# A token product of eight blocks done with seven: sums on GpSimd, copies inside PSUM

## The chip, the cores and the metric

The kernel runs on one core of a Trainium2 chip. The metric is the device time of one execution in microseconds; the time before is the median of three runs. The profile comes from one further execution, whose times are measured by the hardware profiler: its span reaches from the first to the last instruction of the program.

## The reference

Eight batches pass through linear attention with a normalisation for each head, and then through an MLP mixer, in fp32:

```python
kv = np.einsum('bhsd,bhse->bhde', k, v)              # batch 8, heads 8, seq 576, head size 64
out = np.einsum('bhsd,bhde->bhse', q, kv)
rms = np.sqrt(np.mean(out * out, axis=-1, keepdims=True) + 1e-06)
x = (out / rms * g_norm)                             # as (batch 8, seq 576, 512)
xt = x.transpose(0, 2, 1)
h = np.maximum(xt @ w_tok1, 0.0) @ w_tok2            # w_tok1 576 x 256, w_tok2 256 x 576
u = x + h.transpose(0, 2, 1)
h2 = np.maximum(u @ w_ch1, 0.0) @ w_ch2              # w_ch1 512 x 1536, w_ch2 1536 x 512
return u + h2
```

The change touches the product `xt @ w_tok1`, the first token product. All weights arrive as 64-bit floats; the kernel turns them into fp32 on ScalarE and VectorE, which its text calls rounding.

## The kernel before

The batches are taken in four pairs. Of each pair there are nine tiles of 128 rows and 512 columns: four tiles of the first batch (side 0), four of the second (side 1), and a ninth that holds the last 64 rows of both. They are kept two by two as X[pair, c], with c from 0 to 4: X0 and X1 are side 0, X2 and X3 side 1, X4 the ninth tile. For each pair the kernel does

- **attention**: the key-value products (`kv`, evicted by ScalarE with `e`), then a product for each chunk c (`a0` to `a4`) into two PSUM banks. VectorE multiplies the banks by g_norm into X (the gain, `g`), ScalarE squares them (`q`), VectorE reduces the squares (`t`) and takes the mean (`m`), ScalarE the root (`r`), VectorE the inverse in four small steps (`i`). Then each tile is scaled by the inverse: `s` does one tile in eight ScalarE instructions, `d` one tile on VectorE (`scale_vector`), `p` one tile on GpSimd (`scale_pool`). Chunks are normalised in groups: 0 with 1, 2 with 4, and 3 alone;
- **the first token product** (`h00`, `h01`, `h10`, `h11`, function `tok1`): for each side and each half of the 256 outputs, four matmuls of 128x512 that sum over the four row tiles of that side, in a PSUM bank of pool `h` (four banks). Then `hr` (`tok1_rem`) adds the remainder's 64 rows to all four banks, and ScalarE writes the relu of each into `h1[side]`;
- **the second token product** (`u0` to `u8`, function `tok2`): two matmuls a tile. For tiles 2, 4 and 6 a bank has been seeded with x by a ScalarE copy (`z`), and the sum is copied back to x by ScalarE; for the others VectorE adds bank and x. GpSimd's queue starts the stores of the finished tiles; behind `u8` it starts three, those of the ninth tile.

The order of all this is written out by hand, as strings of step names in `middle` and `steady`, which `play` goes through. `middle` holds the attention of the second pair beside the mixing of the first; `steady[0]` and `steady[1]` hold that of the third and fourth beside the mixing of the second and third. A name with a minus belongs to the attention of the pair that is being mixed (its last chunk, `-a3`, and its last steps). A bare `1` plays the next step of the rounding of the channel weights: a clamp, a shift or an addition on VectorE, where the shift's step also issues the next block's two scaling activations on ScalarE. `f` fetches the next block of channel weights, `x` transposes finished tiles on VectorE (`turn_early`, four transposes) into parts of w_ch2 that are not filled yet, and `b` stores them; `l`, `lq` and `lr` load keys and values, queries, and their remainders on SyncE's queue.

All instructions keep the order in which the steps issue them, on each engine (`keep`). Matmuls are recorded by a helper on line 136, additions on 127, copies on 133, relus on 130; line 494 is the gain, 498 the square, 522 the reduction, 527 the mean, 532 the root, 536 to 541 the inverse, 557 the scaling on ScalarE, 566 that on VectorE, 570 that on GpSimd. Lines 181 and 186 are the scaling activations of a block of channel weights, 202, 206 and 211 clamp, shift and addition, 687 the transposes. In the changed program these lines stand one to some 95 lines further on.

Of the kernel before, what the change touches and what calls it, by code (L numbers as in the profile page):

```python
# [11 lines left out]
F32 = mybir.dt.float32  # L12
# [3 lines left out]
ALU = mybir.AluOpType  # L16
# [4 lines left out]
def kernel(  # L21
# [32 lines left out]
    nc = tc.nc  # L54
    P = 128
    B, S, DM = k.shape
    D = g_norm.shape[0]
# [13 lines left out]
    NU = B + 1  # L71
    NG = 1 + B // 2
    T = 2 * P
    assert B // 2 == 4
    EPS = 1e-6
    TOP = (2.0 - 2.0 ** -3 - 2.0 ** -23) * 2.0 ** -96

# [37 lines left out]
    def do(f, *a, **kw):  # L115
        return lambda: f(*a, **kw)
# [6 lines left out]
    def dma(o, i, engine=nc.sync):  # L123
        keep(engine.dma_start(o, i))

    def tensor_add(o, a, b, op=ALU.add, engine=nc.vector):
        keep(engine.tensor_tensor(out=o, in0=a, in1=b, op=op))  # L127

    def relu(o, a):
        keep(nc.scalar.activation(o, a, AF.Relu))  # L130

    def copy(o, a):
        keep(nc.scalar.copy(o, a))  # L133

    def matmul(*a, **kw):
        keep(nc.tensor.matmul(*a, **kw))  # L136
# [120 lines left out]
    def get_ch2(f):  # L257

        def loads(raw):
            t = raw.rearrange("p (f n) w -> p f n w", f=2)  # L260
            rows = words(moe_w_ch2)[ts(f, 2 * P)].rearrange("(f p) n w -> f p n w", f=2)
            return [(t[:, i], rows[i]) for i in range(2)]

        dst = w_ch2[:, 2 * f // NS, ds(2 * f % NS, 2)]
        return block(2 * DM, loads, dst.rearrange("p f h n -> p (f h n)"), True)
# [117 lines left out]
    def x_of(pair, i):  # L383

        return X[pair, i // 2][:, i % 2]

    def attention(pair, groups):
# [155 lines left out]
        def inv_of(c, t):  # L543

            if alone(c):
                return stat[t][2].rearrange("p (k h) o -> p k h o", h=2)
            inv = stats_of(c)[2]
            if whole:
                return inv[:, t].rearrange("p (k h) o -> p k h o", h=2)
            return inv[:, :, ts(t, HP)].rearrange("p h k o -> p k h o")  # L550
# [12 lines left out]

        def scale_vector(c, t):
            x = X[pair, c][:, t].rearrange("p (k h d) -> p k h d", h=2, d=D)
            keep(nc.vector.tensor_mul(x, x, inv_of(c, t).to_broadcast([P, HP, 2, D])))

        def scale_pool(c, t):
            x = X[pair, c][:, t].rearrange("p (k h d) -> p k h d", h=2, d=D)
# [25 lines left out]
        return steps  # L595


    def token_mixing(pair, seeds, aside=()):
        h1, acc = {}, {}

        def tok1(side, t, js=range(J)):
            if js[0] == 0:
                acc[side, t] = ps["h"].tile([P, DM], F32, name="ps_h", tag="h")
            for j in js:
                matmul(acc[side, t], lhsT=w_tok1[j // 2][:, j % 2, ts(t, P)],
                                 rhs=x_of(pair, side * J + j), start=(j == 0), stop=False)

        def tok1_rem():
            for t in range(NTOK):
                for side in range(2):  # L610
                    r = ds(side * HF, HF)
                    matmul(acc[side, t], lhsT=w_tok1r[r, ts(t, P)],
                                     rhs=x_of(pair, 8)[r], start=False, stop=True)
            for side in range(2):
                h1[side] = hp_.tile([P, NTOK, DM], F32, name="h1", tag="h1")
                for t in range(NTOK):
                    relu(h1[side][:, t], acc[side, t])

        def seed(i):


            acc[i] = ps["h"].tile([P, DM], F32, name="ps_u", tag="h")
            copy(acc[i], x_of(pair, i))

        def tok2(i):
            if i not in seeds:
                n = "o" if i in aside else "h"
                acc[i] = ps[n].tile([P, DM], F32, name="ps_u", tag=n)
            first = i not in seeds
            if i < 8:  # L630
                for t in range(NTOK):
                    matmul(acc[i], lhsT=w_tok2[:, t, ts(i % J, P)], rhs=h1[i // J][:, t],
                           start=(first and t == 0), stop=(t == NTOK - 1), skip_group_check=True)
            else:
                for t in range(NTOK):
                    for side in range(2):
                        matmul(acc[i][ds(side * HF, HF)], lhsT=w_tok2[:, t, LO:],
                               rhs=h1[side][:, t],
                               start=(first and t == 0), stop=(t == NTOK - 1), skip_group_check=True)
            x = x_of(pair, i)  # L640
            if first:
                tensor_add(x, acc[i], x)
            else:
                copy(x, acc[i])
            if i == 8:
                dma(u_rest[ts(pair, P)], x, nc.gpsimd)
                for side in range(2):
                    dma(out[2 * pair + side, LO:], x[ds(side * HF, HF)], nc.gpsimd)
            elif i % 2 == 1:
                dma(  # L650
                    u_rows(2 * pair + i // J)[ds((i % J - 1) * P, 2 * P)]
                    .rearrange("(t p) e -> p t e", p=P), X[pair, i // 2], nc.gpsimd)

        steps = {f"h{s}{t}": do(tok1, s, t) for s in range(2) for t in range(NTOK)}
        steps |= {f"h{s}{t}{j}": do(tok1, s, t, (j,)) for s in range(2) for t in range(NTOK) for j in range(J)}
        steps |= {f"z{i}": do(seed, i) for i in seeds}
        return steps | {"hr": tok1_rem} | {f"u{i}": do(tok2, i) for i in range(9)}


# [659 lines left out]
    def play(lines, after={}, **stages):  # L1319

        for name in " ".join(lines).split():
            if name.isdigit():
                for _ in range(int(name)):
                    next(stages["rounding"], lambda: None)()
            elif name[0] == "-":
                stages["before"][name[1:]]()
            else:
                next(stages[s][name] for s in ("attention", "mixing", "more")  # L1330
                     if name in stages.get(s, ()))()
# [3 lines left out]
    tok2 = [get_tok2(t) for t in range(NTOK)]  # L1335
    first_rows = [get_tok1_half(j) for j in range(2)]
    channel = ([get_ch1(c, f) for f in range(2) for c in range(NC)]
               + [get_ch2(f) for f in range(NF // 2)])
    dma(g_row, bass.AP(tensor=g_norm.tensor, offset=g_norm.offset, ap=[[0, 1], list(g_norm.ap[0])]), nc.gpsimd)
    load(0)  # L1340
    first_rows[0][0]()
# [32 lines left out]
    def spread_g():  # L1374
# [12 lines left out]
    middle = [  # L1387
        "h100 h110 h101 h111 w31 w22 w23 w24", "kv00 e00 -lq1 w32 w33 w34",
        "h102 h112 h103 h113 w41 w42 w43 w44", "kv01 e01", "hr l0 z2",
        "a0 q00 g01 q01 g00 t00 t01", "u0 f0", "u1 z4", "u2", "a1 q10 g11 q11 g10",  # L1390
        "kv10 kv11 e10 e11 t10 t11 m0 r0 lq0", "u3 z6 i0 d00 s01 d11 f1", "u4 l1", "a2 q20 g21 q21 g20",
        "a4 q40 t20 g41 q41 t21 g40 lr0 lr1", "u5 s10 t40 t41 m2 r2 f2 1", "u6 1 i2 p20 p21 x00", "u7 1 1"]
    steady = [[
        "kv00 kv01 e00 e01 -d40 f3", "-u8 -a3 -q30 -g31 -q31 -g30 -t30 -t31 -m3 -r3 -lq1",
        "h00 -i3 -d31 -s30 l0 b00 1 1", "h01 f4 x01 1", "a0 q00 g01 q01 g00", "h10 t00 t01 b01 x10 1",
        "h11 1 x11 1", "hr z2 f5 f6", "a1 q10 g11 q11 g10 lq0", "kv10 kv11 e10 e11 t10 t11 m0 r0", "u0 i0 1",
        "u1 z4 d00 s01 l1", "u2", "a2 q20 g21 q21 g20", "a4 q40 t20 g41 q41 t21 g40 lr0 lr1", "u3 z6 d11 1",
        "u4 s10 t40 t41 m2 r2 1 f7", "u5 i2 d20 p21 1 1", "u6 1 f8", "u7 1 1 b10 b11"], [
        "kv00 kv01 e00 e01 -d40 f9", "-u8 -a3 -q30 -g31 -q31 -g30 -t30 -t31 -m3 -r3 -lq1",
        "h00 -i3 -d31 -s30 x20 1", "h01 x21 1", "a0 q00 g01 q01 g00", "h10 t00 t01 1 1", "h11 f10 1 1", "hr z2",  # L1400
        "a1 q10 g11 q11 g10", "kv10 kv11 e10 e11 t10 t11 m0 r0", "u0 f11 i0 1", "u1 z4 d00 s01", "u2",
        "a2 q20 g21 q21 g20", "a4 q40 t20 g41 q41 t21 g40", "u3 z6 d11 1", "u4 s10 t40 t41 m2 r2 1",
        "u5 i2 d20 p21 1", "u6 1 f12 b20 b21", "u7 1", "a3 q30 g31 q31 g30", "u8 t30 t31 m3 r3 f13"]]

    attentions = [attention(0, ((0,), (1,), (2,), (3,), (4,)))]
    attentions += [attention(p, ((0, 1), (2, 4), (3,))) for p in range(1, B // 2)]

    mixings = [token_mixing(p, (2, 4, 6)) for p in range(B // 2 - 1)]
    mixings.append(token_mixing(B // 2 - 1, range(2, 9), (0, 1)))
    more = {f"w{n}{k}": f for n, b in enumerate(first_rows[:1] + tok1[1:] + tok2 + first_rows[1:]) for k, f in enumerate(b)}  # L1410
    more |= {f"f{n}": b[0] for n, b in enumerate(channel)}
# [11 lines left out]

    more |= {f"j{n}": do(keep_warm, n) for n in (4, 5, 21)}
    more["gs"] = spread_g
    more |= {f"zk{side}{half}": do(spread_k, side, half) for side in range(2) for half in range(2)}
    more |= {f"zz{side}": do(zero_rows, side) for side in range(2)}
    play(start, attention=attentions[0], mixing=mixings[0], more=more)
    play(middle, attention=attentions[1], mixing=mixings[0], before=attentions[0],
         more=more, rounding=rounding)  # L1430
    for n in range(1, B // 2 - 1):
        play(steady[n - 1], attention=attentions[n + 1], mixing=mixings[n], before=attentions[n] | {"u8": mixings[n - 1]["u8"]},
             more=more, rounding=rounding)


# [113 lines left out]
```

## Time and profile before

| | |
|---|---|
| median of three runs | 769.95 us (769.78 to 770.12) |
| the profiled execution | 770.03 us, span 768.2 us |
| TensorE busy | 761.7 us (99%) |
| VectorE, ScalarE, GpSimd busy | 644.7, 279.8, 112.9 us |
| first token product in the profile | 128 rows of 128x512, 57.6 us, mean 600 ns |

Busy time is given for each engine as a share of the span. A matmul's own duration is longer than the time to the next one's start, since matmuls overlap; what counts for TensorE's queue is the distance from start to start. Each fp32 matmul of the program is two rows in the profile. In a timeline, a row gives the start in us, the duration in us, the engine, the line, the operation, and what it writes and reads; in brackets stands how long the engine was idle before and what ended it.

### The profile page before, as it was taken

How to read it: one execution, taken by the hardware profiler on the slowest of the kernel's cores; microseconds unless marked ns; L12 is line 12 of the kernel's file. 1: busy time of each engine (PE TensorE's matmuls, PEld its weight loads, DVE VectorE, ACT ScalarE, POOL GpSimd, SP SyncE). 2: the span in 40 equal slices, each digit the busy share in tenths (PEclk: the TensorE clock that was granted, in tenths of full speed). 3: DMA queues.
4: the chain of work that ended last, by engine and by line, in shares of the span. 5: the costliest groups of instructions: out<-in, count | busy, mean ns of one | idle time of the engine just before them, and what ended most of it. 6: DMA issues, size and time to landing. Idle time of an engine off the chain costs nothing.

```text
span 768.2 us, 12734 instructions
## 1 busy us (share of the span) xinstructions
PE 761.7 (99%) x4694; PEld 613.6 (80%) x4694; DVE 644.7 (84%) x957; ACT 279.8 (36%) x563; POOL 112.9 (15%) x125
## 2 busy tenths in 40 slices
PE   9999999999999999999999999999999999999997
PEld 8655555446888888888888888888888888888887
DVE  4868886997757779899968989997898997798996
ACT  3656666763210232512234241123352223325221
POOL 1003030204410000002240002042000227000204
PEclk9999999999999999999999999999999999999999
DMA  9999997599699785689997578999659889855679
GB/s 353 375 369 372 379 372 271 174 323 345 243 288 322 290 276 175 180 264 215 223 229 248 155 225 214 263 185 266 193 151 296 160 227 209 202 149 159 150 193 120
DMA packets 137966, 188.28 MB, mean 245 GB/s; under 512 B 48689, under 2 KB 95793, under 8 KB 135857
## 3 DMA queue, kind: packets, MB, share of 16 engines
q1 hardware_dynamic: 102096, 168.59, 69.2%
q0 software_dynamic: 34848, 18.36, 16.2%
q8 instruction: 38, 0.62, 0.3%
q10 hardware_dynamic: 960, 0.52, 0.2%
q14 instruction: 24, 0.19, 0.1%
HBM read 138.28 MB, written 49.15 MB: 244 GB/s over the span
## 4 chain that ended last, share of the span: by engine, by line
PE 96%; DMA 2%; DVE 1%; SPq 0%; issue 0%; ACT 0%; DVEq 0%
PE ps_d L136 28%; PE ps_b L136 19%; PE ps_a L136 19%; PE ps_u L136 8%; PE ps_h L136 8%; PE ps_v L136 5%; PE ps_c L136 3%; PE ps_w L136 2%; PE ps_kv L136 2%; PE ps_o L136 2%; DMA raw<-in_moe_w_tok_dram 1%; DMA v_in<-in_k_dram 1%; PE ps_r L136 0%; DVE x L494 0%; DVE ms L522 0%; DVE w_tok L211 0%
## 5 line engine op out<-in xcount | busy, mean ns | idle before, releaser
L136 PE MATMUL ps_d<-ui,w 128*128 128x256 f32 x504 | 118.6, 379 | 0.0
L136 PEld LDWEIGHTS ps_d<-ui,w 128*128 128x128 f32 x504 | 95.8, 190 | 13.0
L133 ACT COPY ps_d<-ps_a 128x768 f32<-128x768 f32 (+1 forms) x56 | 32.0, 572 | 199.9 <-PE ps_a L136 196.9
L127 DVE TENSOR_TENSOR v<-v,v 128x1536 f32<-128x1536 f32 (+2 forms) x70 | 103.2, 1481 | 0.3
L136 PE MATMUL ps_b<-sv,w 128*128 128x256 f32 x324 | 78.9, 379 | 0.0
L136 PE MATMUL ps_a<-v,w 128*128 128x256 f32 x324 | 78.7, 379 | 0.0
L1273 POOL DMA_DIRECT2D out_dram<-us x24 | 26.8, 1834 | 291.8 <-ACT p L133 286.5
L136 PEld LDWEIGHTS ps_b<-sv,w 128*128 128x128 f32 x324 | 61.2, 190 | 8.9 <-issue 0.6
L136 PEld LDWEIGHTS ps_a<-v,w 128*128 128x128 f32 x324 | 61.6, 190 | 8.4
L136 PE MATMUL ps_u<-h,w_tok 128*128 128x512 f32 (+1 forms) x160 | 64.7, 599 | 0.0
L130 ACT ACTIVATE v<-v 128x768 f32<-128x768 f32 (+1 forms) x54 | 42.6, 822 | 55.1 <-DVE v L127 52.3
L136 PE MATMUL ps_d<-v,w 128*128 128x256 f32 x258 | 62.7, 379 | 0.0
L136 PE MATMUL ps_h<-x,w_tok 128*128 128x512 f32 x128 | 57.6, 600 | 0.7 <-DVE w_tok L211 0.6
L1273 POOL DMA_DIRECT2D out_dram<-r x40 | 41.3, 1924 | 102.0 <-ACT p L133 80.3
L136 PE MATMUL ps_d<-sv,w 128*128 128x256 f32 x228 | 55.4, 379 | 0.0
L136 PEld LDWEIGHTS ps_d<-v,w 128*128 128x128 f32 x258 | 48.9, 190 | 6.6
L136 PEld LDWEIGHTS ps_u<-h,w_tok 128*128 128x128 f32 (+1 forms) x160 | 25.6, 179 | 31.1 <-issue 26.7
L136 PEld LDWEIGHTS ps_d<-sv,w 128*128 128x128 f32 x228 | 43.3, 190 | 5.9
L136 PE MATMUL ps_a<-uT,w 128*128 128x256 f32 x192 | 46.7, 379 | 0.0
L136 PEld LDWEIGHTS ps_h<-x,w_tok 128*128 128x128 f32 x128 | 23.5, 190 | 28.4 <-issue 24.2
L136 PE MATMUL ps_b<-ui,w 128*128 128x256 f32 x168 | 40.8, 379 | 0.0
L136 PEld LDWEIGHTS ps_a<-uT,w 128*128 128x128 f32 x192 | 36.5, 190 | 5.0
(178 smaller groups left out, 1296.7 us busy)
## 6 DMA issues: line engine op xcount, KB each, us to landing
w<-parts SPq DMA_DIRECT2D x168, 384.0 KB
w<-parts SPq DMA_DIRECT2D x56, 192.0 KB
uT<-blocks SPq DMA_DIRECT2D x36, 256.0 KB
k_in<-in_k_dram SPq DMA_DIRECT2D x8, 1024.0 KB
v_in<-in_v_dram SPq DMA_DIRECT2D x8, 1024.0 KB
qT<-in_q_dram SPq DMA_DIRECT2D x8, 1024.0 KB
out_dram<-x POOLq DMA_DIRECT2D x16, 512.0 KB, 6.9
raw<-in_moe_w_ch_dram SPq DMA_DIRECT2D x8, 768.0 KB
```

Of the source, the lines that this page charges most:

```text
L127: keep(engine.tensor_tensor(out=o, in0=a, in1=b, op=op))
L130: keep(nc.scalar.activation(o, a, AF.Relu))
L133: keep(nc.scalar.copy(o, a))
L136: keep(nc.tensor.matmul(*a, **kw))
L1273: keep(nc.gpsimd.dma_start(to, t()[ds(b * Q, Q), at].rearrange("p n l j -> p n (l j)"), accum_op=ALU.add))
```

## The change

For the second and third pair (`fast`) the first token product is taken as a product of 2x2 blocks: the weight's two halves of outputs and two halves of rows, against the rows' halves of both sides. Eight block products become seven (`p1` to `p7`, two matmuls each), in the form with four sums of weight blocks and four of x blocks:

- the four sums of weight blocks (`mix_tok1`, 128x256 each) are made once by GpSimd in `middle`, the four sums of x blocks (`t_sum`, 128x1024 each) by GpSimd for each pair. They lie in two parts of w_ch2 that are not filled yet (`sums_room`, `room`) and in the two h1 tiles. The second sum of a pair waits for the `scale_vector` written last before it (`late["mark"]`);
- `p1` goes into bank a and is copied by ScalarE into bank y; `p6` is added to y, and y copied into bank d; `p3` is added to y, `p7` to d; `p5` has bank b. Banks b and d are copied into h1[0], then `p2` is added to a and `p4` to d;
- the remainder is added in two groups (`ha` to y and a, `hb` to b and d), and h1 is made by two relus from the banks, two VectorE additions of a bank to what was copied into h1[0], and two relus on the spot.

Beside that: tiles 3 and 5 of these pairs are seeded, so their result is a ScalarE copy and no VectorE addition; `p20`, `p21` in `middle` and `p21` in `steady[0]` become `d20`, `d21`, so three tile scalings go from GpSimd to VectorE; the stores of the ninth tile are a step of their own (`v8`) and stand behind two sums; the blocks of w_ch2 are fetched and rounded in the order 1, 2, 4, 5, 0, 3; and rounding steps, transposes and stores of blocks have new places (two rounding steps go from `middle` to `steady[1]`). The core of the diff:

```diff
+        def product(name, lhs, rhs, start=False):
+            if start:
+                h_bank(name)
+            for j in range(2):
+                matmul(bank[name], lhsT=lhs[:, j], rhs=rhs[:, j], start=(start and j == 0),
+                       stop=False, skip_group_check=True)
+
+        def copied(name, of):
+            h_bank(name)
+            copy(bank[name], bank[of])
+
+        def p1():
+            product("a", a_block(0, 0), x_block(11), True)
+            copied("y", "a")
+
+        def p5():
+            product("b", tok_sum(1), room, True)
+
+        def p6():
+            product("y", tok_sum(2), h1[1])
+            copied("d", "y")
+
+        def p3():
+            product("y", tok_sum(4), x_block(22))
+
+        def p7():
+            product("d", tok_sum(3), h1[0])
+            copy(h1[0][:, 0], bank["b"])
+            copy(h1[0][:, 1], bank["d"])
+
+        def p2():
+            product("a", a_block(0, 1), x_block(21))
+
+        def p4():
+            product("d", a_block(1, 1), room)
...
+        def rem_first():
+            rem(0, "ya")
+            relu(h1[1][:, 0], bank["a"])
+            tensor_add(h1[0][:, 0], bank["y"], h1[0][:, 0])
+            relu(h1[0][:, 0], h1[0][:, 0])
...
-        "a4 q40 t20 g41 q41 t21 g40 lr0 lr1", "u5 s10 t40 t41 m2 r2 f2 1", "u6 1 i2 p20 p21 x00", "u7 1 1"]
+        "a4 q40 t20 g41 q41 t21 g40 lr0 lr1", "u5 s10 t40 t41 m2 r2 f2 1", "u6 i2 1 d20 d21 P1 x00", "u7"]
     steady = [[
-        "kv00 kv01 e00 e01 -d40 f3", "-u8 -a3 -q30 -g31 -q31 -g30 -t30 -t31 -m3 -r3 -lq1",
-        "h00 -i3 -d31 -s30 l0 b00 1 1", "h01 f4 x01 1", "a0 q00 g01 q01 g00", "h10 t00 t01 b01 x10 1",
-        "h11 1 x11 1", "hr z2 f5 f6", "a1 q10 g11 q11 g10 lq0", "kv10 kv11 e10 e11 t10 t11 m0 r0", "u0 i0 1",
+        "kv00 kv01 e00 e01 -d40 f3", "-u8 y2 y3 -v8 -a3 -q30 -g31 -q31 -g30 -t30 -t31 x01 -m3 -r3 -lq1",
+        "p1 -i3 -d31 -s30 1 l0 b00 1", "p5 1 f4", "p6", "a0 q00 g01 q01 g00 y4", "p3 t00 t01 b01 x10", "p7 1", "p2 1", "ha 1",
+        "p4 1", "hb z2 z3 f5 f6 1", "a1 q10 g11 q11 g10 lq0", "kv10 kv11 e10 e11 t10 t11 m0 r0", "u0 i0 1 1",
...
+        "-u8 y2 y3 -v8 -a3 -q30 -g31 -q31 -g30 -t30 -t31 x20 -m3 -r3 -lq1",
+        "p1 -i3 -d31 -s30", "p5 1", "p6 1", "a0 q00 g01 q01 g00 y4", "p3 t00 t01 x21", "p7 1", "p2 f10", "ha 1", "p4 1", "hb z2 z3 1 1",
```

## The prediction

> **What bounds the kernel now.** The engine totals come first. TensorE is busy for 761.7 of 768.2 us, so an edit counts by what it takes from TensorE's queue and by what it makes that queue wait for.
>
> ```profile
> span 768.2 us, 12734 instructions
> ...
> PE 761.7 (99%) x4694; PEld 613.6 (80%) x4694; DVE 644.7 (84%) x957; ACT 279.8 (36%) x563; POOL 112.9 (15%) x125
> ```
>
> The busy time by stretches then shows where the 6.5 us of idle TensorE lie. The rows below are the stretches of the edit: the first product of the second and third pair (the second and fourth row), and what is around them. TensorE has no gap in any of them, so what is saved there is saved whole, and each new wait is paid whole. ScalarE has room (8.31 of 17.14 us), VectorE hardly any (16.50).
>
> ```profile
> core 0: us, PE busy (x) PEld busy (x) DVE busy (x) ACT busy (x) POOL busy (x), PEclk, DMA share, GB/s
> ...
> 44.00:70.16 26.16, 26.16 (x491) 15.63 (x489) 18.45 (x40) 16.95 (x44) 4.33 (x5) 1.00 1.02 388
> 70.16:87.30 17.14, 17.14 (x111) 7.63 (x105) 16.50 (x36) 8.31 (x18) 2.42 (x4) 1.00 1.02 383
> 87.30:111.85 24.55, 24.55 (x427) 14.68 (x425) 20.05 (x41) 17.34 (x43) 4.52 (x5) 1.00 1.01 374
> 111.85:129.00 17.15, 17.15 (x112) 7.64 (x107) 13.61 (x30) 9.25 (x20) 1.66 (x3) 1.00 0.97 344
> ```
>
> Third, TensorE's timeline in the first of these stretches: attention (1.09 us from start to start), eight matmuls of the first product, attention, eight more, the remainder.
>
> ```profile
> 69.07 1.16 PE L136 MATMUL ps_o<-kvp,qT 64*64 64x64 f32 x64
> 70.16 7.13 PE L136 MATMUL ps_h<-x,w_tok 128*128 128x512 f32 x16
> 77.22 1.16 PE L136 MATMUL ps_o<-kvp,qT 64*64 64x64 f32 x64
> 78.31 7.13 PE L136 MATMUL ps_h<-x,w_tok 128*128 128x512 f32 x16
> 85.38 1.99 PE L136 MATMUL ps_h<-x,w_tok1r 64*128 64x512 f32 x8
> ```
>
> Each matmul of the program is two rows, and 16 rows take 7.06 us from start to start: 0.441 us a row, 1.765 us for a block product (two matmuls).
>
> Last, ScalarE and VectorE beside it. Nothing of ScalarE is needed soon by TensorE here, and its queue stands for microseconds behind VectorE. The row to look at is the root (L532): it comes 5.2 us after the attention that it belongs to has left TensorE, since it needs two gains, two squares, two reductions and the mean.
>
> ```profile
> 70.34 0.60 ACT L498 ACTIVATE sq<-ps_o 128x512 f32<-128x512 f32 x1 [0.81 <-PE ps_o L136]
> ...
> 75.41 0.21 ACT L532 ACTIVATE root<-ms 128x16 f32<-128x16 f32 x1 [1.34 <-DVE ms L527]
> 76.65 2.02 ACT L557 ACTIVATE x<-x,inv 128x64 f32<-128x64 f32 x8 [1.02 <-DVE inv L541]
> 78.57 0.90 ACT L181 ACTIVATE w_ch<-raw 128x768 f32<-128x768 f32 x1
> 79.38 0.91 ACT L186 ACTIVATE raw<-raw 128x768 uint32<-128x768 uint32 x1
> ```
>
> **What the change removes.** Eight block products become seven: two matmuls, four rows, in each of two pairs: 8 x 0.441 = 3.53 us off TensorE. The remainder's eight rows (1.92 us) stay but stand in two groups; I add 0.1 us a pair (0 to 0.25; the same rows can't get cheaper by being parted).
>
> **What it makes TensorE wait for.** The sixth product (p6) adds onto a bank that ScalarE fills with the first (p1), and p3 may write that bank only when ScalarE has copied it on. ScalarE works in its written order, which in the changed program is, for the second pair:
>
> ```
> square, square (attention a3)    root [waits VectorE's mean]
> copy first product -> bank y     [p6 waits for it]
> scale x 8 [waits the inverse]    two activations of a weight block
> copy bank y -> bank d            [p3 waits for it]
> ```
>
> So the copy that p6 needs stands behind the root. TensorE leaves a3, does p1 and p5 (3.53 us) and is at p6. VectorE's way to the root has grown by four transposes (x01, x20) put ahead of the mean.
>
> Third pair first, where VectorE has no backlog by then: its queue before a3 (the scales, four transposes, two adds) is done about when a3 ends. From a3's end: first gain 0.1 to 0.75, second after the first square 1.35, reductions to 2.55 (0.6 each), transposes 1.28 to 3.85, mean to root's end 0.43, copy 0.58 (with 0.13 from the root's start to the next row). The copy ends 4.8 after a3, TensorE is there after 3.53: a stall of 1.3. A restart adds 0.15: the four rows that start at 27.85 after the one listed wait of ps_h take 1.92 us to the next start, not 1.77. Together 1.45 (1.2 to 2.3).
>
> Second pair: VectorE is late. From the root of the group before (done 65.45) its queue is inverse 1.0, clamp 0.5, two scales that were GpSimd's 1.2, transposes 1.28, add 0.6: 70.0. Then comes the scale d40, which reads two SBUF tensors while GpSimd makes its first sum. The rows show that the two engines exclude each other: a clamp that takes 0.56 took 1.42 and ended 0.4 us after GpSimd's multiplication.
>
> ```profile
> 68.00 2.07 POOL L570 TENSOR_TENSOR x<-x,inv 128x512 f32<-128x512 f32 x2 [2.39 <-DVE inv L541]
> ...
> 105.98 1.56 POOL L570 TENSOR_TENSOR x<-x,inv 128x512 f32<-128x512 f32 x1
> 106.53 1.42 DVE L202 TENSOR_SCALAR w_ch<-w_ch 128x768 f32<-128x768 f32 x1
> ...
> 182.78 1.01 POOL L127 TENSOR_TENSOR sv<-w_ch 128x384 f32<-128x384 f32 x1
> ```
>
> No row has GpSimd's sum of 128x1024. Bounds: two of 128x512 with a spread operand, 2.07, and the 128x384 row scaled, 2.67. I take 2.4, as the 384 row has two full operands but carries its start-up. The first sum then runs from 68.25 to 70.65, d40 to 71.2, the add 71.8, gains 73.0, reductions 74.2, transposes 75.5, mean and root 75.9, copy 76.4. TensorE is at p6 at 70.16 + 3.53 = 73.69: 2.75, with the restart 2.9. Low end 1.45 (third pair's chain), high end 4.35: at 2.67 a sum, GpSimd's third sum lasts until 77.0, and the mean waits for it.
>
> The Trainium skill's "GPSIMD Engine Reference" (section 3.1) gives 4497 ns for a sum of 2048 elements a partition; half of that is an estimate of 2.25 us, by which the sum below would be 0.15 lower.
>
> p3 in the second pair: after the root 1.0 for the inverse, 1.92 for eight scales, 1.61 for the two activations, then the copy 0.57: 5.1 after the root's end. TensorE after the root's end: copy 0.5, p6 1.92, a0 1.09, so it is there at 3.5: 1.6 and the restart, 1.8 (1.3 to 2.3). In the third pair the two activations stand behind the copy, and it is ready as TensorE comes: 0.2 (0 to 0.6).
>
> **What is covered.** GpSimd's sums: p5's ends at 70.65 and is needed at 71.93, p6's at 73.8, before p6's copy; p7 and p4 come later still. If these covers fail it is GpSimd's excess, under 1 us. Behind a sum that waits (the second for d40, the fourth for a3's scaled tile) stand only stores of finished tiles, and those tiles are overwritten a whole pair later. ScalarE's further copies (h1 twice, two more seeds and results, 0.58 each) lie beside 3.6 us of attention and key-value matmuls between the remainder and the first u: the last relu ends 1.5 to 2 us after the remainder. Behind a relu that waits for VectorE's add stand a1's squares, and a second gain waits for the first of them; nobody on TensorE waits for these before the next attention. VectorE gives four adds to ScalarE and gets four: nothing; its three scales from GpSimd (0.6 each) are in the chains above. The later weight order and the later stores of the ninth tile move no load that TensorE is near: keys and values are asked for some 33 us ahead (70.74 for 106.56). In the last stage VectorE is full from 139 to 181.5, but two adds fewer stand in it, so it keeps up with an earlier TensorE; I cost it at nothing (0 to 0.5).
>
> **Sum**, on the profiled execution's 770.03 (span 768.2), 0.1 above the median 769.95: -3.53 + 2.9 + 1.8 + 1.45 + 0.2 + 0.2 = +3.0, so 773.0. All low ends give 770.4, all high ends 777.0.
>
> A rule that speaks against the change: the Trainium skill's "TensorE: Matmul & The Clock Gate" (Part 1) halves TensorE's clock after an idle window of about 3.4 us. The rows grant 1.00 throughout, with gaps no longer than 1.1 us in the waits, so they can't show it; by the rule only p6's high end would be touched, by an estimated 1.7 us more.
>
> **Rivals.** (a) Faster: p1's copy is made in time, the saving lands whole and 766.7 is read. It needs the stalls of both pairs together to stay under 1.7 us (770.03 - 3.53 + 0.2 is 766.7, and 768.4 is where faster begins). For it: ScalarE is idle for half of these stretches. Against it: its idle time is this very wait for VectorE, and the chain without backlog already gives 1.3 a pair. (b) No change: p6 waits 1.45 in each pair, as VectorE is as early in the second as in the third, and p3 finds its copy made; with the 0.2 of the remainder -0.4, 769.6. Against it: the 1.6 us of scaling activations stand ahead of that copy. (c) Beyond the forecast: GpSimd's sums hold VectorE's small two-input steps in both pairs; two more sums' ends of 1.2 each, 775.4.
>
> **How the numbers follow.** Within 0.2% (1.5 us, about what a measurement can tell) of 769.95 is no change. Forecast with (c) 0.70, (b) 0.15, (a) 0.15. The forecast's lower tail (0.05) lies within the 1.5 us, so faster 0.15, same 0.19, slower 0.66. The forecast's own range is 770.4 to 777.0; holding 8 in 10, with most of (b), is 769.5 to 775.8.
>
> **What would show it.** TensorE: four rows of ps_h fewer a pair, a gap ahead of p6 in both pairs (2.9 and 1.45 us, ended by a ScalarE copy that starts right after the root), a gap of 1.8 ahead of p3 in the second pair alone. GpSimd: 128x1024 rows of 2.1 to 2.7. Wrong would be: no gap at p6, or the root within 2.5 us of a3's end; then it is faster.

## The result, and the profile after

The changed kernel takes 773.75 us (median of five runs, 773.52 to 774.82), the kernel before in the same comparison 770.12 us (769.78 to 770.89). The ratio is 1.0048, with a 95% interval of 1.0034 to 1.0063: slower by 3.6 us where 3.0 were forecast. The profiled execution takes 773.52 us (span 771.5), 3.5 more than that of before.

The engine totals of the changed kernel say that TensorE has 1.3 us less to do, in a span that is 3.3 us longer:

```profile
PE 760.4 (99%) x4686; PEld 612.5 (79%) x4686; DVE 648.5 (84%) x960; ACT 287.5 (37%) x579; POOL 130.5 (17%) x134
```

TensorE's list of waits (total, times, longest, in us) has two entries that before has not. The first is the copies inside PSUM. The second is a gap in the attention remainder (`ps_r`, 32 rows) that no engine's step ends, in the word of the profile an `issue`:

```profile
PE ps_h L137 <- ACT ps_h L134: 4.4, 3, 1.7
PE ps_r L137 <- issue: 1.1, 1, 1.1
```

```profile
58.90 0.41 PE L137 MATMUL ps_r<-kvp,qR 64*64 64x64 f32 x15
60.44 0.50 PE L137 MATMUL ps_r<-kvp,qR 64*64 64x64 f32 x17 [1.14 <-issue]
```

The busy time by the same stretches as before (first product of the second pair in the second row, of the third in the fourth):

```profile
44.27:71.51 27.24, 26.10 (x490) 15.75 (x488) 20.35 (x43) 15.34 (x41) 6.93 (x8) 1.00 1.00 378
71.51:90.87 19.36, 16.13 (x107) 6.62 (x101) 16.32 (x31) 12.26 (x25) 8.45 (x6) 1.00 1.00 374
90.87:115.42 24.55, 24.55 (x426) 14.68 (x425) 21.13 (x43) 17.49 (x45) 6.13 (x6) 1.00 1.00 346
115.42:132.68 17.26, 16.05 (x106) 6.62 (x100) 12.90 (x28) 10.84 (x23) 7.78 (x6) 1.00 0.56 196
```

Before, they were 26.16, 17.14, 24.55 and 17.15 long. So the second pair's product has lost 2.2 us, the third pair's 0.1, and the stretch ahead of both 1.1, by the gap without a releaser. Everything behind keeps its length: TensorE's last row ends at 768.12, before at 764.41. That is 3.7 us later: these 3.4, and 0.3 by which the first of the stretches starts later. The span grows by 3.3 only, since what follows TensorE's last row took 3.4 us here and 3.8 before.

TensorE's timeline in the second pair's product, from p1 to p3:

```profile
71.51 1.99 PE L137 MATMUL ps_h<-x,w_tok 128*128 128x512 f32 x4
73.33 1.88 PE L137 MATMUL ps_h<-w_ch 128*128 128x512 f32 x4
76.93 1.95 PE L137 MATMUL ps_h<-h,w_ch 128*128 128x512 f32 x4 [1.72 <-ACT ps_h L134]
78.81 1.16 PE L137 MATMUL ps_o<-kvp,qT 64*64 64x64 f32 x64
81.49 1.98 PE L137 MATMUL ps_h<-x,w_ch 128*128 128x512 f32 x4 [1.51 <-ACT ps_h L134]
```

Where p1 and p5 run into p6 it starts 3.54 us after p1 (third pair of the first experiment), so p6 is 1.88 us late and p3, due 1.09 after a0's start, 1.59. In the third pair p6 is 1.37 us late (120.33, p1 at 115.42) and p3 has no gap. ScalarE's timeline ahead of the second pair's p6:

```profile
76.08 0.22 ACT L533 ACTIVATE root<-ms 128x16 f32<-128x16 f32 x1 [3.02 <-DVE ms L528]
76.20 0.58 ACT L134 COPY ps_h<-ps_h 128x512 f32<-128x512 f32 x1
```

The copy that p6 waits for starts right behind the root, and the root comes 4.6 us after the attention a3 has left TensorE. VectorE's mean ahead of it starts at 75.45 and takes 0.60 us; it ends just after GpSimd's third sum (73.64 + 2.36 = 76.00). In the third pair, where that sum is over by then (116.88 + 2.35 = 119.23), the mean takes 0.13. The sum and the mean, first in the second pair, then in the third:

```profile
73.64 2.36 POOL L128 TENSOR_TENSOR h<-x 128x1024 f32<-128x1024 f32 x1
...
75.45 0.60 DVE L528 TENSOR_SCALAR ms<-ms 128x16 f32<-128x16 f32 x1
...
116.88 2.35 POOL L128 TENSOR_TENSOR h<-x 128x1024 f32<-128x1024 f32 x1
...
119.31 0.13 DVE L528 TENSOR_SCALAR ms<-ms 128x16 f32<-128x16 f32 x1
```

### The profile page after: what moved, and what is told of

It reads as the page before. It is cut to its first block, busy times and chain, and to the rows that moved or that the text cites. A ratio compares the mean times of both kernels' runs of the same rounds, so it can differ in the third digit from the quotient of the medians.

```text
span 771.5 us, 12763 instructions
## 1 busy us (share of the span) xinstructions
PE 760.4 (99%) x4686; PEld 612.5 (79%) x4686; DVE 648.5 (84%) x960; ACT 287.5 (37%) x579; POOL 130.5 (17%) x134
## 4 chain that ended last, share of the span: by engine, by line
PE 92%; DVE 4%; DMA 2%; ACT 1%; issue 0%; SPq 0%; DVEq 0%; ACTq 0%
PE ps_d L137 28%; PE ps_b L137 19%; PE ps_a L137 19%; PE ps_u L137 7%; PE ps_h L137 6%; PE ps_v L137 5%; PE ps_c L137 3%; PE ps_w L137 2%; PE ps_kv L137 2%; DMA raw<-in_moe_w_tok_dram 1%; PE ps_o L137 1%; DMA v_in<-in_k_dram 1%; DVE x L495 1%; DVE ms L523 1%; DVE w_ch L781 1%; ACT x L558 0%
## 5 line engine op out<-in xcount | busy, mean ns | idle before, releaser
L128 DVE TENSOR_TENSOR v<-ps_b,u 128x768 f32<-128x768 f32 x28 | 26.8, 956 | 15.6 <-PE ps_b L137 12.5
L134 ACT COPY u<-ps_d 128x256 f32<-128x256 f32 (+1 forms) x44 | 23.2, 528 | 43.4 <-PE ps_d L137 43.4
```

The lines of the kernel that those rows point to most:

```text
L128: return keep(engine.tensor_tensor(out=o, in0=a, in1=b, op=op))
```

## The experiments

"Before" in each comparison is the kernel before on the same chip (medians 770.02 to 770.22).

**1. The copies first.** Only step names in the two strings move:

```diff
-"... -t30 -t31 x01 -m3 -r3 -lq1", "p1 -i3 -d31 -s30 1 l0 b00 1", "p5 1 f4", "p6", "a0 ...
+"... -t30 -t31", "p1 x01 -m3 -r3 -lq1", "p5", "p6 -i3 -d31 -s30 1 l0 b00 1 1 f4", "a0 ...
-"... -t30 -t31 x20 -m3 -r3 -lq1", "p1 -i3 -d31 -s30", "p5 1", "p6 1", "a0 ...
+"... -t30 -t31", "p1 x20 -m3 -r3 -lq1", "p5", "p6 -i3 -d31 -s30 1 1", "a0 ...
```

> ScalarE's two copies are put ahead of what they stood behind (the first ahead of the root, the second right behind the root and ahead of the scales and the rounding), in both pairs; nothing else moves. Queue theory (the copies are late because of what stands ahead of them on ScalarE, so TensorE's gaps ahead of p6 and p3 are these and nothing more): the gaps of 1.9 and 1.6 us in the second pair and of 1.3 us in the third go, 4.8 us in all; 773.6 becomes 768.8, a little under the kernel before (767.5 if the gap of 1.1 us in the attention remainder is not there). Rival, GpSimd's sums decide: p6 and p7 then wait for the second and third sum instead, 1 us or more in each pair, 771 to 772. Rival, the moved steps beside the products cost the time: no less than 771.5. The gap in the attention remainder comes again if it belongs to the program, since the instructions up to it are the same in the changed kernel; it is away in some of these runs if it is chance.

Measured: 771.69 us (1.0008 to 1.0026 times before). All the gaps ahead of p6 and p3 are gone, in both pairs: the copies were late because of what stood ahead of them on ScalarE. But 2.9 us more were expected to go. TensorE's timeline shows a new gap ahead of p4, and the four rows behind it take 2.94 us from start to start in place of 1.92:

```profile
85.70 3.02 PE L137 MATMUL ps_h<-w_ch,w_tok 128*128 128x512 f32 x4 [2.34 <-ACT h L134]
88.64 1.71 PE L137 MATMUL ps_h<-x,w_tok1r 64*128 64x512 f32 x4
```

p4 waits for ScalarE's copies of banks b and d into h1, and these stand behind a0's second square, which waits for VectorE's gains; VectorE is held up by a rounding addition that takes 2.47 us beside GpSimd's fourth sum (0.96 alone):

```profile
79.52 2.36 POOL L128 TENSOR_TENSOR w_ch<-x,h 128x1024 f32<-128x1024 f32 x1 [1.87 <-ACT x L558]
...
80.23 2.47 DVE L212 CUSTOM_DVE_ANT_1 w_ch<-w_ch,raw 128x1536 uint16<-128x1536 uint16 x1 [1.71 <-ACT w_ch L182]
```

The slow rows are a halved clock, told of below. Its price shows in the times too: of the eleven executions three have a mean granted clock of 0.999 or 1.000 and take 770.7 to 770.9 us, eight have 0.997 or 0.998 and take 771.6 to 772.2.

**2 and 4. The transposes behind the root; and the third sum behind the mean as well.**

```diff
-... -t30 -t31 x01 -m3 -r3      (steady[0]; x20 in steady[1])
+... -t30 -t31 -m3 -r3 x01
```

> The four transposes x01 and x20 that the change put ahead of the mean are put behind the root again, in both pairs; all else is as in the changed kernel. Queue theory, as the prediction had it (the transposes are 1.28 us of VectorE's way to the root): the root comes 1.3 us earlier in each pair, p6's gaps go from 1.9 and 1.3 to 0.6 and 0.1 us, 773.6 becomes 771.1. Rival, GpSimd's third sum holds the mean (it lasts from 73.64 to 76.00 in the second pair and from 116.88 to 119.23 in the third, and the mean ended 0.05 and 0.2 us after it): the mean is ready 1.3 us earlier but is done only when the sum ends, the root moves by 0.2 us at most, the time stays at 773.4 to 773.6, and the mean's row takes up to 1.9 us in place of 0.60 and 0.13.

```diff
-            if n == 2:                       # t_sum: the sum that waits for VectorE
-                tc.add_manual_dep(i.ins, late["mark"].ins.name, ...)
+            if n in (2, 3):
+                tc.add_manual_dep(i.ins, late["mark" if n == 2 else "mean"].ins.name, ...)
-... y2 y3 -v8 ... -m3 -r3 x01
+... y2 -v8 ... -m3 y3 -r3 x01
```

> As the run with the transposes behind the root, and besides GpSimd's third sum is made to wait for the mean, in both pairs. Queue theory: the sum makes no difference, 771.1 like the run without it. Rival, GpSimd's third sum holds the mean: only now does the root come 1.3 us earlier; p6's gaps fall from 1.9 and 1.3 us to 0.3 and 0.1, 773.6 becomes 770.8, while the run without this one edit stays at 773.5. The gap of 1.6 us ahead of p3 in the second pair stays by both.

Measured: 775.27 us with the transposes moved, 777.56 with the sum moved too; both slower than the changed kernel, against either theory's time. The rows say why. First the kernel with the transposes moved, then the one with both edits (second pair):

```profile
73.57 2.34 POOL L128 TENSOR_TENSOR h<-x 128x1024 f32<-128x1024 f32 x1
74.04 1.92 DVE L528 TENSOR_SCALAR ms<-ms 128x16 f32<-128x16 f32 x1
```

```profile
74.32 0.17 DVE L528 TENSOR_SCALAR ms<-ms 128x16 f32<-128x16 f32 x1
...
75.38 1.96 PE L137 MATMUL ps_h<-h,w_ch 128*128 128x512 f32 x4 [1.38 <-ACT ps_h L134]
75.51 2.37 POOL L128 TENSOR_TENSOR h<-x 128x1024 f32<-128x1024 f32 x1
...
75.99 1.93 DVE L538 SCALAR_TENSOR_TENSOR ms<-ms,inv 128x16 f32<-128x16 f32 x1
```

With the transposes out of the way the mean is at the head of VectorE's queue 1.4 us sooner, and is held until the sum ends: 1.92 us for 16 elements a partition. The root comes at 75.99 in place of 76.08. And the transposes now stand ahead of the inverse, so the scales start 0.84 us later (78.16) and p3 waits 0.83 us in the third pair, where it had no gap; in the second, p6's wait of 3.11 us brings the halved clock. With the sum behind the mean, the mean takes 0.17 and p6 starts 1.5 us sooner than in the changed kernel; but the same sum then holds the second small step of the inverse for 1.93 us (0.17 alone), and behind the inverse stand the scales and the copy that p3 needs: its gap grows to 4.16 us. So GpSimd's third sum is as long a way to the root as VectorE's queue with its transposes: with the transposes alone out of the way p6 starts 0.1 us sooner in the second pair and, counted from p1, 0.2 in the third, and with the sum out of the way as well the hold moves to the inverse. The sum moved alone was not run; by the rows the mean, at 75.45, could have ended at most 0.5 us sooner.

**3. The rounding behind p6** in the second pair, so that the copy y to d comes right after the scales:

```diff
-"p1 -i3 -d31 -s30 1 l0 b00 1", "p5 1 f4", "p6", "a0 ...
+"p1 -i3 -d31 -s30 l0 b00", "p5 f4", "p6 1 1 1", "a0 ...
```

> In the second pair alone the weight block's rounding that stood between p1 and p6 is put behind p6, so that ScalarE makes the copy y to d right after its eight scales. Queue theory: the gap of 1.6 us ahead of p3 goes, p6's stays; 773.6 becomes 772.0. Rival, the copy is late for another reason (the scales, or GpSimd): p3 still waits 1 us or more and the time stays within 0.5 of 773.6. Rival, VectorE is full, so the block that now comes later is late for its own use: the gap goes and comes back somewhere before the last stage, 773 to 774.

Measured: 773.51 us (1.0027 to 1.0055). The gap ahead of p3 is gone, as expected, and the time has not moved. In this execution the gap in the attention remainder is away: TensorE is at p6 1.4 us sooner, p6 starts at 76.96 all the same (76.93 in the changed kernel), and has waited 3.13 us. Then TensorE runs slowly. Its busy time and granted clock (the figure after the busy times) in three stretches of 3.41 us:

```profile
74.63:78.04 3.41, 1.08 (x3) 0.63 (x4) 2.99 (x10) 1.38 (x5) 3.01 (x4) 1.00 1.03 406
78.04:81.46 3.42, 3.42 (x67) 1.85 (x65) 0.81 (x3) 3.11 (x9) 1.94 (x1) 0.50 1.02 423
81.46:84.87 3.41, 3.41 (x14) 1.63 (x9) 3.38 (x5) 1.79 (x4) 0.43 (x1) 1.00 0.93 369
```

For one stretch the clock is half. p6 and a0 take 2.63 and 1.92 us where they take 1.88 and 1.09, and that makes up what the missing gap ahead of p3 gave. The five executions agree with this: four with a mean granted clock of 0.997 or 0.998 take 773.40 to 773.53 us, and the one with 0.999 takes 772.63.

**8. The changed kernel once more.**

> The changed kernel once more, unaltered. Theory: the gap of 1.1 us in the attention remainder is chance and costs nothing, since p6 waits for VectorE's chain, whose end does not move with TensorE: without the gap p6 waits 3.1 us in place of 1.7, the granted clock halves for 3.4 us after it, and p3 hardly waits; the time is 773.5 to 774.0 as in the first run. Rival, the gap belongs to this program and the time contains it: it comes again, with p6's wait at 1.7 and the clock at 1.00.

Measured: 773.74 us. The gap in the attention remainder is 0.25 us this time, p6 waits 2.60, p3 1.50, and the time is the same. So in the profiled execution neither of the two descriptions holds whole: the gap does vary from execution to execution, and costs next to nothing, as p6 starts when the copy comes (76.93, 76.96 and 77.09 with gaps of 1.14, none and 0.25); but the clock stayed up. The wait was cut by the edge of a 3.41 us stretch, and TensorE was busy for 1.51 us of the second part:

```profile
75.19:78.60 3.41, 1.51 (x4) 0.68 (x4) 2.99 (x9) 1.82 (x7) 2.58 (x4) 1.00 1.05 416
```

The profiled executions are not typical in this. Of the changed kernel's ten executions (five here, five in the first comparison) three have a mean clock of 1.000 and take 773.5 to 773.8 us, four 0.997 or 0.998 and take 773.6 to 773.8, three 0.995 and take 774.8 to 775.0. One halved stretch of 3.41 us lowers the mean by 0.002, so by this estimate the four had one and the three had two. One costs nothing here, as the theory had it, with p3's wait to take it up; two cost 1.2 us. Where they fell no profile shows.

**5. What stands beside the products, alone.** The strings of the changed kernel with `h00` to `hr` in place of `p1` to `hb`, no sums (`fast = ()`), and `z3`, `z5` left out.

> The eight block products as before, without GpSimd's sums, the spread banks and the two extra seeds, but with all that the change moves beside them (VectorE's scales in place of GpSimd's, the transposes ahead of the mean, the order of the stores and of the later weights, the places of the rounding). Theory: the moved steps lengthen VectorE's queue, which TensorE doesn't wait for here, so 770.1 within 0.4. Rival, the moved steps cost by themselves: 771 or more, and what is told of the copies is short by as much.

Measured: 770.19 us, ratio 0.9991 to 1.0009. The scales on VectorE, the transposes' places, the stores and the order of the weights cost nothing by themselves, so the 771.7 of experiment 1, which its last rival had named as well, is not theirs.

**6. The copies first, and the rounding later.** As experiment 1, and

```diff
-"p6 -i3 -d31 -s30 1 l0 b00 1 1 f4", ... "ha 1", ... "u1 z4 d00 s01 l1 1", ... "u3 z6 d11",
+"p6 -i3 -d31 -s30 l0 b00", ... "ha 1 f4", ... "u1 z4 d00 s01 l1 1 1", ... "u3 z6 d11 1 1",
```

> As the run with the copies first, and besides the three rounding steps of the second pair that stood between p1 and p6 are put behind the remainder, among the u products, so that VectorE comes to a0's gains 4 us earlier. Theory: in the run with the copies first TensorE lost 2.3 us ahead of p4 to ScalarE's copies of the banks b and d, which stood behind a0's second square, and that behind VectorE's gains and a rounding that GpSimd's fourth sum held; and 1.7 us more to the halved clock after it. Both go: 771.7 - 2.3 - 1.7 = 767.7, the clock stays at 1.00 to the last stage, and both pairs give their 1.77 us: faster than before by 2.4 to 3.4. Rival, VectorE is full and the rounding that now comes later holds a gain or an add further on: a gap of 1 to 2 us at the u products or the next attention, 769 to 770. Rival, GpSimd's fourth sum is late for p4: the gap stays.

Measured: 768.96 us, 0.9973 to 0.9991 times before: faster than both kernels. The gap at p4 and the slow clock are gone; a gap of 0.58 us has come ahead of a u product, so the first rival has a share. But gaps alone do not make up the difference to the 767.7 expected: TensorE's rows in the third pair have none, and the stretch is 15.82 us long, 1.33 under the 17.15 of before, not 1.67. In its timeline the last block product parts the remainder:

```profile
121.64 1.88 PE L137 MATMUL ps_h<-x,w_tok 128*128 128x512 f32 x4
123.45 1.13 PE L137 MATMUL ps_h<-x,w_tok1r 64*128 64x512 f32 x4
124.51 1.98 PE L137 MATMUL ps_h<-w_ch,w_tok 128*128 128x512 f32 x4
126.42 1.13 PE L137 MATMUL ps_h<-x,w_tok1r 64*128 64x512 f32 x4
```

(a1 follows at 127.48.) A product with its own kind behind it takes 1.72 us from start to start (p7, 119.92 to 121.64), one with a change of kind on one side 1.81 or 1.82 (p2, 121.64 to 123.45), one with a change on both sides 1.92 (124.51 to 126.42).

**9. The remainder together.** p4 ahead of both remainder groups, in both pairs:

```diff
-"p2 1", "ha 1 f4", "p4 1", "hb z2 z3 f5 f6 1"      (steady[1] likewise)
+"p2 1", "p4 1 f4", "ha 1", "hb z2 z3 f5 f6 1"
```

> As the run with the copies first and the rounding later, and besides the last block product p4 is put ahead of the remainder's first group, so that the eight remainder rows stand together again, in both pairs. Theory: a change between matmuls of 128 and of 64 rows costs TensorE about 0.1 us on each side; two such changes fewer a pair take back the 0.40 us by which the remainder grew (2.32 in place of 1.92 us for eight rows), so 769.0 - 0.8 = 768.2. Rival, the rows themselves are dearer (other banks): no change, 769.0. Rival, the relus that now come later hold the first u product: a new gap there of 0.5 us or more, 769 or more.

Measured: 770.28 us (0.9994 to 1.0012). The remainder's rows confirm the theory: eight take 1.91 us again, and TensorE's way from p3 to a1 is 8.98 and 9.05 us in place of 9.38 in both pairs. The time went up nonetheless. ScalarE's seeds of the u products now come too late, with gaps of 1.60 us in the second pair and 0.96 in the third; in the second pair they stand behind squares that wait for VectorE's gains. The second rival had named the u products, but not the cause: it is not the relus that are late, but the attention that stands between the u products.

**10. The rounding last**, the three steps at the end of the second pair's u products:

```diff
-"u1 z4 d00 s01 l1 1 1", ... "u3 z6 d11 1 1", ... "u6 f8", "u7 b10 b11"
+"u1 z4 d00 s01 l1 1", ... "u3 z6 d11", ... "u6 f8 1", "u7 b10 b11 1 1"
```

> As the run with the remainder together, and the three rounding steps of the second pair go to its last two u products instead of its second and fourth. Theory: the gap of 0.58 us ahead of a u product, in which a seed's copy on ScalarE stood behind VectorE's gains, and those behind the rounding, goes: 768.2 - 0.7 = 767.5, with no gap on TensorE in either pair. Rival, the work meets the third pair's chain instead (d40, the first sum, the gains) and TensorE waits at p5 or p6 there: 768.0 or more.

Measured: 770.73 us (1.0002 to 1.0020). The rival holds: no gap in the second pair, but in the third p6 waits 1.27 us for GpSimd's sum and p4 0.74 for ScalarE's copy, and 0.99 follow at its u products.

**12. The rounding spread**, one step from the second u product to the fifth, on the kernel of experiment 6:

```diff
-"u1 z4 d00 s01 l1 1 1", ... "u4 s10 t40 t41 m2 r2 f7 1"
+"u1 z4 d00 s01 l1 1", ... "u4 s10 t40 t41 m2 r2 f7 1 1"
```

> As the run with the copies first and the rounding later, with one of the three displaced rounding steps moved on from the second u product to the fifth. Theory: the gap of 0.58 us ahead of the seventh u product stood behind the rounding's two activations on ScalarE, which came between the attention's gains and squares there; it goes and 769.0 becomes 768.3, 0.2% under the kernel before. Rival, the work meets the third pair's first sums or the u products behind: a gap of 0.5 us or more elsewhere, 768.9 or more.

Measured: 768.98 us, the same as experiment 6. The gap of 0.58 us is gone and one of 0.80 stands in the third pair's u products.

**7 and 11. The third pair alone** with seven products and the copies first (`fast = (2,)`, `steady[0]` nearly as before: with the third pair's first sum, one scale on VectorE and one rounding step fewer):

> The second pair with eight products as before, the third pair with seven and the copies first. Theory: the third pair waits for nothing (no gap in the run with the copies first) and gives its 1.77 us whole: 770.1 - 1.77 + 0.1 = 768.4. Rival, the saving is given back later, by VectorE or the stores of the last stage: 769.5 or more.

Measured: 772.04 us. Two gaps, 1.35 us at the third pair's u products and 1.81 within the last pair's first token product (behind the scales of a3, which wait for VectorE). This kernel had one more rounding step done by the third pair's end than the changed one. Without it:

```diff
-"u6 1 i2 p20 p21 x00", "u7 1 1"      (middle, as in the kernel before)
+"u6 1 i2 p20 p21 x00", "u7 1"
```

> The second pair with eight products as before, the third with seven and the copies first, with as many rounding steps done by each pair's start as in the changed kernel but for one (the earlier run of this had one too many, so that the larger blocks of the second weight were rounded a step sooner). Theory: the saving of one pair measured alone: 4 rows less 0.40 us for the split remainder, 1.3 us, no gap in the third pair or behind it: 770.2 - 1.3 = 768.9. Rival, the seven products of the third pair press VectorE against the last stage whatever the rounding does: gaps of 1.4 and 1.8 us come again, 771 to 772.

Measured: 768.86 us, 0.9977 to 0.9995 times before. One rounding step decides between 1.2 us under and 1.8 us over the time before. The profiled execution of this kernel (769.77 us) has the gap in the attention remainder, 0.86 us, and no long wait behind it that could take it up; most of its other runs lie at 768.7 to 768.9. Seven products in both pairs (experiment 6, 768.96) end no lower than seven in the third pair alone.

## Why the prediction was right, and where its steps were off

The order of the result was right, and so was the mechanism that carried it: TensorE stops at p6 and p3 for copies that stand behind the root, the scales and the rounding. Experiments 1, 3 and 6 show it, each gap going with the edit that was to remove it. The terms, one by one:

- **Four rows fewer a pair** were sized at 0.441 us a row. Rows in a run are 0.429 apart (1.72 for four), so 3.43 in place of 3.53: the 0.441 had the changes of kind at both ends of the sixteen rows in it.
- **The split remainder** is the step that was most wrong for its size: 0.1 a pair, 0.25 at most, against 0.40 (9.38 to 8.98 us with the groups together). I took only parting into account, not that each change between matmuls of 128 and of 64 rows costs.
- **p6 in the second pair**, 2.9: 1.88 in the profiled execution, where TensorE came to p1 1.35 us later than before (71.51 against 70.16), 1.1 of them by the gap in the attention remainder. With that gap small or away it is 2.76 (77.09, p1 at 70.79, experiment 8) and 3.3 (76.96, p1 at 70.13, experiment 3). The end of the wait was forecast at 76.4, and came at 76.93 to 77.09.
- **What sets that end** was half seen. The chain through VectorE with four more transposes is there. Equal to it stands GpSimd's third sum, which I had at the high end alone and, in rival (c), as something on top. My own 2.4 us a sum put the end of that sum at 76.0 (71.2 and two sums), where it came, and by the steps of the high end that makes 3.35 in place of 2.9; the sum of the forecast left it out. It isn't on top: the two ways end within half a microsecond of each other, and by that luck the term came near with one of its two causes missing (experiments 2 and 4).
- **p3 in the second pair**, 1.8: 1.59. **p6 in the third**, 1.45: 1.37. **p3 in the third**, 0.2: nothing.
- **The restart**, 0.15 in three of these terms: 0.07 for p6 (1.88 to the next start after the wait, 1.81 without one, experiment 6) and nothing for p3 (1.82 both times). The four rows at 27.85 that it was read from stand between rows of other kinds, and 1.92 is what a block with a change on both sides takes without any wait (p4, experiment 6).
- **GpSimd's sum**, 2.4: 2.36. The estimate of 2.25 from the Trainium skill's "GPSIMD Engine Reference" (section 3.1) is 0.11 short of it.
- **The side moves and the last stage** at nothing: nothing (experiment 5; the last stage keeps its length).

By experiment 8 the terms make -3.43 + 0.8 + 2.76 + 1.58 + 1.37 = +3.1; 3.5 were measured in that comparison. Most of the rest is the gap in the attention remainder in that execution: 0.5 us (59.07 to 60.15 from the remainder's start to u's, where before has 58.94 to 59.52). Without the gap, p6's term is 3.3 and the same sum 3.6. So the 3.0 came near as a sum of errors: the remainder was 0.6 too small in both pairs together, p6 in the second pair 0.4, and the other terms together 0.4 too large. The clock, which the prediction let touch the high end alone, halves, by their mean clock, in seven of the changed kernel's ten executions (experiment 8), at a price of nothing to 1.2 us.

Rival (a) was the one that an edit of order alone can bring nearer, but none of the orders tried reached its figure of 766.7: experiments 6, 11 and 12 end at 768.9 to 769.0. Where TensorE comes earlier, ScalarE and VectorE beside the u products are late, and the two edits that took a gap away there (experiments 10 and 12) brought one elsewhere. Whether a better order of the rounding exists stays open.

Also open is why the gap in the attention remainder comes. It was 1.14, 0.25 and 0.86 us in three profiled executions and away in the eleven others, among them kernels with the same instructions up to that place, so those instructions alone do not decide it. The traces do show what goes with it. The longer of the two queues of instruction packets (q8, 16 KB each) has one packet just before this place. Where the gap is, the packet lands at 59.12, 58.33 and 58.73 us, and the gap ends 1.3, 1.4 and 1.3 us after that, each time with the sixteenth row. In the eleven others it lands at 55.3 to 57.3, 1.9 us or more ahead of that row. So the gap looks like a wait for instructions that came late; no run changes the packet's time, and what delayed it stays open.

## What to carry to other kernels

A copy between two engines' steps costs what stands ahead of it in its engine's queue, not its own 0.58 us: read that queue back to its last wait on a third engine before counting the saving. Where two chains end together, shortening one gives next to nothing, so look for the one that ends second before making an experiment of it. And on an engine whose neighbours are nearly full, time saved can come back as gaps further on, as it did here; the order that fitted the old pace has to be made again.

## What was not expected of the hardware

**The clock.** The prediction said that gaps of up to 1.1 us cannot show the clock gate. These runs show it. After the waits of 2.34, 3.11, 3.13 and 4.16 us (experiments 1, 2, 3 and 4) the granted clock was 0.50 for 3.41 us, in each. It starts not with the gap but at the edge of a stretch of 3.41 us. Every change of the granted clock in a trace lies a whole number of such stretches from the others, so the edges are known where the clock does not change too. Counted so, TensorE had been idle for 2.34, 2.11, 2.33 and 2.53 us of the stretch before the halved one, and for 1.90 in experiment 8, 1.72 in the changed kernel's first run and 1.81 in experiment 4's third pair, where the clock stayed at 1.00. These idle times are no threshold: where TensorE's work ends, stretches with 1.82 and 1.74 us idle (experiment 2, 767.63 to 771.04; experiment 4, 769.54 to 772.96) were followed by 0.50. The Trainium skill's "TensorE: Matmul & The Clock Gate" (Part 1) has the free-running window of 3413 ns, and the runs agree with that. It names an idle window of that length as the condition; here windows in which TensorE was busy for 0.9 to 1.3 us were enough. By where the edge fell, a wait of 2.60 us cost nothing more (experiment 8), and one of 3.13 us made the rows behind it 1.6 us longer (experiment 3).

**GpSimd and VectorE.** A sum of 128x1024 on GpSimd held a mean of 128x16 for 1.92 us and a small two-input step for 1.93, while a reciprocal of 128x16 (0.21), transposes and gains from PSUM ran beside it at their usual length. The Trainium skill's "SBUF — State Buffer" (Who interferes with whom) says it of instructions with two SBUF inputs and of tensor-scalar instructions in a two-port mode. The small step has two such inputs and agrees; whether the mean ran in that mode no trace here shows. In a chain of tiny steps one that is held takes nearly as long as the sum, however small it is.

**TensorE's rows.** A change between matmuls of 128 and 64 rows adds about 0.1 us on each side: in experiment 6 the rows stand 0.52 to 0.53 us apart at the change and 0.429 within a run of 128.
